# An mLSTM and mixture-of-experts kernel: its opening in a new order, with the scores of four tiles in paired row halves

## Chip, cores and metric

The kernel runs on one core of a Trainium2 chip, in one launch that computes the whole chain of three layers. The metric is the device time of one execution in microseconds (us); the median over several runs is given. The layout of the inputs (transposed copies, the gates repeated for each row group, the weights in blocks) is made on the host ahead of the launch and is not part of the time.

## The reference, cut to what is computed

Sizes: B=2 sequences of S=768 tokens, 8 heads of 40 columns, so 1536 tokens of 320 columns. First comes an mLSTM attention step by step over the tokens, then a mixture of 4 experts (320 to 1024 and back), then a gated feed-forward layer (320 to 1536 and back).

```python
def _attn_ref(q, k, v, i_gate, f_gate, o_gate):
    m = np.full((B, H), -1e+30)            # C, n start at zero
    for t in range(S):
        kt, vt, qt = k[:, :, t], v[:, :, t], q[:, :, t]
        m_new = np.maximum(f_gate[:, :, t] + m, i_gate[:, :, t])
        f_stab = np.exp(f_gate[:, :, t] + m - m_new)
        i_stab = np.exp(i_gate[:, :, t] - m_new)
        m = m_new
        C = f_stab * C + i_stab * np.einsum('bhd,bhe->bhde', vt, kt)
        n = f_stab * n + i_stab * kt
        h_tilde = np.einsum('bhde,bhe->bhd', C, qt)
        denom = np.maximum(np.abs(np.einsum('bhd,bhd->bh', n, qt)), 1.0)
        y[:, :, t] = sigmoid(o_gate[:, :, t]) * h_tilde / denom
    return y

def _moe_ref(x, domain_probs, w1, w2):
    p = domain_probs / (domain_probs.sum(-1, keepdims=True) + 1e-09)
    for e in range(E):
        out += p[:, e:e + 1] * (np.maximum(x @ w1[e], 0.0) @ w2[e])
    return out

def _moe2_ref(x, w_a, w_b, w_out):
    return ((x @ w_a) * (x @ w_b)) @ w_out
```

## The kernel before, in words

**Tiles.** The tokens are cut into 12 tiles of 128, numbered n = 2j+b: j (0 to 5) is the stretch of 128 tokens and b the sequence. Both tiles of one j go through the main products together, as 256 columns. The step-by-step attention is done in chunks: within a tile as a 128x128 matrix of scores times weights for each head, and from tile to tile through a state that is carried on.

**Attention of one tile.** The gates of a stretch j give running sums (gate0 and gate1 L379 to L389, gate_f L393 to L396, gate_i L400, gate2 L402 to L409, gate_c L415). Their result L is split into a rounded part (hi_L, hi_cm, L429) and a rest (low_L L442, low_cm L446). build_R (L475 to L482) spreads it over the heads in the tile's buffer Rr, four heads at a time ("half" hh = 0 or 1 of a tile); the lower rows of Rr are filled once (fill_R, L670). weights_of (L486 to L492) is one TensorE product of LT and Rr, w_exp (L497) its exponent on ScalarE, w_mask (L505) the causal mask on GpSimd. scores (L507 to L513) are four products of keys and queries in fp32, on 120 rows: for tiles 0 and 1 64 rows come from memory, and rows 64 to 120 are set to zero (zero_qk, L336); tiles 2 and 3 use the same buffers again and load 40 rows over them. s1b (L517, VectorE) multiplies scores and weights, s2a (L519 to L527) multiplies by the values, s2x (L550 to L562, VectorE) divides and applies the output gate og, whose sigmoid is o_gate (L362). s2c (L610, ScalarE) copies the last 64 columns of x once more, s3a (L145 to L147) transposes x on TensorE, and x_hi (L133, ScalarE) and x_lo (L136 and L138, VectorE) split it into a rounded and a rest part, xh and xl. Later tiles (from j=2 on) get their weights another way and are not touched by the change.

**Main products.** The 72 items k = 0 to 71 stand for the products of expert weights and both tiles of one j, twelve items for each j (blocks 0 to 2 of the weights, four items a block; the other blocks follow after them for all tokens). Item k multiplies into psa (L208, eight products of 256 columns), VectorE and ScalarE split the result (L275 and L276), and the second product goes into psy (L287 to L289). Two pieces of 352 columns of weights feed an item; block 0 thus has eight pieces, f = 0 to 7. A piece is a small generator (piece1): the first step is a load (L87, 176 KB, queue SP), the second ScalarE's rounded copy (L91), the third the subtraction that gives the rest (L93), on VectorE or on GpSimd after a table (block 0: p p v p v v p p, block 1: p p p v p p p v, p for GpSimd). A pass of `go` takes each named piece one step further.

**Order.** Everything beside the main products is a list `ev` of (key, function, arguments), L679 on. It is sorted by its keys and issued in that order: keys below zero ahead of item 0 (the opening), a key of 2.4 within item 2. Each engine takes its instructions strictly in the order of issue, and each DMA queue (SP's for most loads, ScalarE's for some, GpSimd's for one kind) its loads. So an instruction that waits holds all behind it on its engine. warm_up (L626) issues products of zeros on TensorE, ten at first and one to four at a time further on. table (L633) is a tiny activation that has ScalarE load the table of a function. weigh_k (L571, GpSimd), state and state_add carry the state on.

The lines that matter most ahead of item 0 are these; the opening of the list before is in the diff below.

## Time and profile before

| | |
|---|---|
| time, median of 3 runs | 612.29 us (611.9 to 612.41) |
| span of the profiled execution | 609.31 us |
| TensorE (PE) busy | 598.1 us, 98% |
| VectorE (DVE) busy | 406.5 us, 67% |
| ScalarE (ACT) busy | 277.9 us, 46% |
| GpSimd (POOL) busy | 193.3 us, 32% |
| granted TensorE clock, slices of the page | 9 tenths or more in all 40 |

The span is that of the profiled execution, from its first instruction to its last; the runs' times include a little more around it, 2.98 us against the median. The shares are means over the whole span. The opening (up to 20.9 us) and the first items are a small part of it, so what happens there is read from the timeline of these stretches, not from the shares. The page's chain of work that ended last is TensorE's for 92% of the span.

### The profile page before, as it was taken

How to read it: one execution, taken by the hardware profiler on the slowest of the kernel's cores; microseconds unless marked ns; L12 is line 12 of the kernel's file. 1: busy time of each engine (PE TensorE's matmuls, PEld its weight loads, DVE VectorE, ACT ScalarE, POOL GpSimd, SP SyncE). 2: the span in 40 equal slices, each digit the busy share in tenths (PEclk: the TensorE clock that was granted, in tenths of full speed). 3: DMA queues.
4: the chain of work that ended last, by engine and by line, in shares of the span. 5: the costliest groups of instructions: out<-in, count | busy, mean ns of one | idle time of the engine just before them, and what ended most of it. 6: DMA issues, size and time to landing. Idle time of an engine off the chain costs nothing.

```text
span 609.3 us, 14397 instructions
## 1 busy us (share of the span) xinstructions
PE 598.1 (98%) x5815; PEld 564.5 (93%) x5815; DVE 406.5 (67%) x829; ACT 277.9 (46%) x643; POOL 193.3 (32%) x233
## 2 busy tenths in 40 slices
PE   8799999999999999999999999999999999999997
PEld 5699999999999899999999999988898988888886
DVE  6898868676553333333789899898776787864344
ACT  7687476756533323333344344454553434331211
POOL 5486426363501011334233333333222222310000
PEclk9999999999999999999999999999999999999999
DMA  8877463737202122222222222222111120200002
GB/s 247 214 219 202 128 181 103 197 104 200 58 19 64 39 62 80 72 75 79 56 76 69 63 75 56 59 63 65 47 50 45 38 56 20 60 16 1 2 31 100
DMA packets 29351, 51.63 MB, mean 85 GB/s; under 512 B 3485, under 2 KB 18117, under 8 KB 29285
## 3 DMA queue, kind: packets, MB, share of 16 engines
q1 hardware_dynamic: 15925, 26.32, 15.9%
q10 hardware_dynamic: 12448, 22.03, 13.2%
q0 software_dynamic: 912, 2.36, 1.4%
q8 instruction: 45, 0.74, 0.5%
q14 instruction: 21, 0.17, 0.1%
HBM read 47.92 MB, written 2.00 MB: 82 GB/s over the span
## 4 chain that ended last, share of the span: by engine, by line
PE 92%; DVE 3%; POOL 1%; issue 1%; DMA 1%; ACT 1%; SPq 0%; DVEq 0%; POOLq 0%
PE psy L253 27%; PE psa L228 27%; PE psb L228 11%; PE psa L208 10%; PE psy L287 3%; PE psy L289 3%; PE psy L288 3%; PE pt_y L527 3%; PE pt_c L513 1%; PE pt_i L533 1%; POOL wl L93 1%; PE pt_u L583 1%; DMA acc<-in_w1b 1%; PE pt_x L145 0%; DMA gt<-in_gates 0%
## 5 line engine op out<-in xcount | busy, mean ns | idle before, releaser
L228 PE MATMUL psa<-xh,wh 64*128 64x512 f32 x576 | 135.2, 390 | 0.0
L253 PE MATMUL psy<-wl,hh 64*128 64x320 f32 x752 | 131.3, 305 | 0.0
L253 PE MATMUL psy<-wh,hh 64*128 64x320 f32 x752 | 131.3, 305 | 0.0
L253 PE MATMUL psy<-wh,hl 64*128 64x320 f32 x752 | 131.2, 305 | 0.0
L228 PE MATMUL psa<-xh,wl 64*128 64x512 f32 x414 | 97.4, 389 | 0.0
L253 PEld LDWEIGHTS psy<-wh,hh 64*128 64x128 f32 x752 | 85.7, 184 | 0.8
L228 PEld LDWEIGHTS psa<-xh,wh 64*128 64x128 f32 x576 | 80.9, 184 | 5.9 <-issue 0.9
L253 PEld LDWEIGHTS psy<-wl,hh 64*128 64x128 f32 x752 | 85.5, 184 | 0.8
L253 PEld LDWEIGHTS psy<-wh,hl 64*128 64x128 f32 x752 | 85.7, 184 | 0.0
L228 PE MATMUL psa<-xl,wh 64*128 64x512 f32 x384 | 85.6, 389 | 0.0
L828 DVE SCALAR_TENSOR_TENSOR hl<-psa,hh 128x512 fp32r<-128x512 f32 x60 | 38.6, 685 | 55.2 <-ACT hh L827 54.9
L125 POOL TENSOR_TENSOR wl<-tp,lf 128x272 fp32r<-128x272 f32 x48 | 38.8, 809 | 113.1 <-DVE tp L124 111.4
L228 PE MATMUL psb<-xh,wh 64*128 64x512 f32 x216 | 69.8, 389 | 0.0
L228 PEld LDWEIGHTS psa<-xh,wl 64*128 64x128 f32 x414 | 60.7, 184 | 3.7
L228 PE MATMUL psb<-xh,wl 64*128 64x512 f32 x180 | 58.5, 389 | 0.0
L228 PEld LDWEIGHTS psa<-xl,wh 64*128 64x128 f32 x384 | 55.2, 184 | 3.6
L122 POOL TENSOR_TENSOR lf<-lf,sq 128x272 f32<-128x272 f32 x48 | 38.1, 794 | 62.9 <-ACT wh L121 48.9
L276 DVE SCALAR_TENSOR_TENSOR hl<-psa,hh 128x256 fp32r<-128x256 f32 x72 | 30.3, 421 | 40.4 <-ACT hh L275 40.0
L93 POOL TENSOR_TENSOR wl<-raw,wh 128x352 fp32r<-128x352 f32 x28 | 26.4, 947 | 95.1 <-ACT wh L91 68.6
L275 ACT ACTIVATE hh<-psa 128x256 fp32r<-128x256 f32 x72 | 27.6, 383 | 59.2 <-PE psa L208 58.5
L827 ACT ACTIVATE hh<-psa 128x512 fp32r<-128x512 f32 x60 | 32.6, 596 | 44.7 <-PE psy L253 26.6
L208 PE MATMUL psa<-xh,wh 128*128 128x256 f32 x216 | 51.5, 293 | 0.3 <-ACT xh L133 0.3
(146 smaller groups left out, 1435.1 us busy)
## 6 DMA issues: line engine op xcount, KB each, us to landing
raw<-in_w2b ACTq DMA_DIRECT2D x48, 272.0 KB, 2.8
...
```

The lines of the kernel that those rows point to most:

```text
L93: lo_eng.tensor_tensor(wl[:, cs], raw, wh[:, cs].bitcast(F32), op=ALU.subtract)
L122: nc.gpsimd.tensor_tensor(lf, lf, sq, op=ALU.mult)
L125: nc.gpsimd.tensor_tensor(wl[:, cs], tf, lf, op=ALU.add)
L208: nc.tensor.matmul(ps, l, r, start=(i == 0), stop=(i == len(prs) - 1))
L228: return nc.tensor.matmul(ps[g], w[rows, o:o + P], x, start=start, stop=stop)
L253: ms = [nc.tensor.matmul(ps[t], l[rows, t * P:(t + 1) * P], w[rows, off:off + DM], start=start, stop=stop) for t, rows in zip(two, (UP, DN))]
L275: nc.scalar.activation(self.hh, ps, AF.Relu)
L276: nc.vector.scalar_tensor_tensor(self.hl, ps, 0.0, self.hh.bitcast(F32), op0=ALU.max, op1=ALU.subtract)
L287: nc.tensor.matmul(ps, lh, wh[:, off:off + DM], start=(fi == 0), stop=False)
L288: nc.tensor.matmul(ps, lh, wl[:, off:off + DM], start=False, stop=False)
L827: nc.scalar.activation(hh, ps[f], AF.Relu)
L828: nc.vector.scalar_tensor_tensor(hl, ps[f], 0.0, hh.bitcast(F32), op0=ALU.max, op1=ALU.subtract)
```

## The change

The list's opening is written anew, and some of the functions it calls are changed:

- **Loads.** The keys and queries of tiles 0 to 3 are loaded as 48 rows a half (RQ), both halves of a tile in one buffer, one from partition 0 and one from partition 64; there is no zero_qk any more. The loads for the second halves of tiles 0 and 1 go on ScalarE's queue. og of j=0 is the third load on SP's queue, ahead of tile 1's first half.
- **Scores.** scores2(n) issues the eight products of a tile's two halves in turns, the one from rows 0 to 39, the other from rows 64 to 103, each into a bank of its own. It serves tiles 0 to 3. Tile 2's stand ahead of item 0, tile 3's at 5.343.
- **ScalarE.** Sigmoid's table is loaded first, then both fills of Rr, then the sigmoid of og 0, then hi_L, then Exp's table. The exponents of tiles 0 and 1 stand in a row of four. Exp's table is not asked for between a sigmoid and the exponents of the next gates in the opening; the entry at 0.678 stays.
- **Gates to GpSimd.** hi_cm of j=0 goes from ScalarE to GpSimd, and so does the first half of tile 1's Rr; the four slices of Rr that ScalarE made go to VectorE as one build of four heads.
- **x of tiles 0 and 1.** The quotient goes into a buffer of its own (xu), and GpSimd multiplies its last 64 columns by og a second time into x; ScalarE's copy of these columns (s2c) is not called for j=0.
- **Moves.** gate0, gate1 and gate_f of j=1 stand in the opening. The first ten warm_up products stay, the later ones go. All pieces of block 0 are done ahead of item 0, w1's first two pieces get both further steps at 1.21 to 1.24. gate_tail 1 goes from 2.939 to 3.8, gate_out 1 from 3.684 to 3.85.

The functions:

```diff
@@ load_qk @@
-            if 2 <= n < NP:
-                t["qk", hh] = td[n - 2]["qk", hh]
+            if n < NP:
+                if "two" not in t:
+                    tag, bufs = ("qs", 2) if n == NP - 1 else ("qk", QB)
+                    t["two"] = qp.tile([KS, 2, 512], F32, tag=tag, name="qk_t", bufs=bufs)
+                at, r, to = 64 * hh, RQ, t["two"]
             else:
-                tag, bufs = ("qs", 2) if (n, hh) == (1, 1) else ("qk", QB)
-                t["qk", hh] = qp.tile([KS, 2, 512], F32, tag=tag, name="qk_t", bufs=bufs)
-            v = t["qk", hh].rearrange("p a b -> p (a b)")
-            r = 64 if n < 2 else D if n < NP else KS
-            (eng or nc.sync).dma_start(v[0:r], qk[n, hh, 0:r])
+                to = t["qk", hh] = qp.tile([KS, 2, 512], F32, tag="qk", name="qk_t", bufs=QB)
+                at, r = 0, KS
+            v = to.rearrange("p a b -> p (a b)")
+            (eng or nc.sync).dma_start(v[at:at + r], qk[n, hh, 0:r])
@@ scores2, new @@
+        def scores2(n):
+            t = td[n]
+            for hh in range(2):
+                t["pc", hh] = ps_t.tile([P, 512], F32, tag="t", name="pt_c")
+            for h in range(4):
+                hs = slice(h * P, (h + 1) * P)
+                for hh in range(2):
+                    v = t["two"][64 * hh:64 * hh + D]
+                    nc.tensor.matmul(t["pc", hh][:, hs], v[:, 1, hs], v[:, 0, hs], start=True, stop=True, skip_group_check=True)
@@ s2x @@
-            nc.vector.tensor_tensor(xv, y[:, :, 0:D], dn.to_broadcast([P, H, D]), op=ALU.mult)
-            t["last"] = nc.vector.tensor_tensor(xv, xv, r, op=ALU.mult).ins
+            if j == 0:
+                xu = a2.tile([P, H, D], F32, tag="y", name="xu_t", bufs=1)
+                nc.vector.tensor_tensor(xu, y[:, :, 0:D], dn.to_broadcast([P, H, D]), op=ALU.mult)
+                nc.vector.tensor_tensor(xv, xu, r, op=ALU.mult)
+                nc.gpsimd.tensor_tensor(x[:, DM:], xu.rearrange("p h d -> p (h d)")[:, 256:DM], og[j][:, b, 256:DM], op=ALU.mult)
+            else:
...
```

The opening of the list (loads of constants and most pieces of weights left out):

```diff
-            (-110, load_gates, 0, nc.sync), (-109, load_rsel, nc.scalar), (-108, load_qk, 0, 0, nc.sync), (-107, load_qk, 0, 1, nc.scalar),
-            (-106, load_qk, 1, 0, nc.sync), (-105, load_qk, 1, 1, nc.sync), (-102.626, zero_qk, 0, 0, V), (-100.942, table, AF.Exp),
...
-            (-68, scores, 0, 0), (-66.868, go, w0[5:6]), (-65.844, scores, 0, 1), (-65.387, gate1, 0),
...
-            (-62.277, hi_cm, 0, nc.scalar), (-62.241, low_L, 0), (-61.301, load_gates, 1), (-60.985, build_R, 0, V, 0, 4), (-60.522, low_cm, 0),
-            (-59.112, build_R, 1, V, 4, 8), (-57.494, build_R, 1, V, 0, 4), (-57.303, fill_R, 1), (-56.721, load_qk, 2, 1),
-            (-56.674, build_R, 0, nc.scalar, 4, 8), (-55, weights_of, 0, 0, ps_b, "b"), (-55, w_exp, 0, 0), (-55, w_mask, 0, 0),
...
+            (-40, load_gates, 0, nc.sync), (-39.9, load_rsel, nc.scalar), (-39.8, load_qk, 0, 0, nc.sync), (-39.7, load_qk, 0, 1, nc.scalar),
+            (-39.6, load_o, 0, nc.sync), (-39.5, load_qk, 1, 0, nc.sync), (-39.4, load_qk, 1, 1, nc.scalar), (-39.3, load_kvo, 1), (-39.2, load_kvo, 0),
+            (-39.1, load_v, 0), (-39, table, AF.Sigmoid), (-38.9, ones), (-38.8, fill_R, 0), (-38.7, fill_R, 1), (-38.6, gate0, 0), (-38.5, warm_up, WARM),
...
+            (-35, scores2, 0), (-34.9, o_gate, 0), (-34.8, gate1, 0), (-34.7, gate_f, 0, V), (-34.6, gate_i, 0, nc.gpsimd), (-34.5, gate2, 0),
+            (-34.4, gate_c, 0, V), (-34.3, hi_L, 0, nc.scalar), (-34.2, hi_cm, 0, nc.gpsimd), (-34.1, low_L, 0), (-34, table, AF.Exp),
+            (-33.9, low_cm, 0), (-33.8, build_R, 0, V, 0, 4), (-33.7, build_R, 1, nc.gpsimd, 0, 4), (-33.6, build_R, 0, V, 4, 8), (-33.5, build_R, 1, V, 4, 8),
+            (-33.4, scores2, 1), (-33, weights_of, 0, 0, ps_b, "b"), (-32.9, w_exp, 0, 0), (-32.8, w_mask, 0, 0), (-32.7, weights_of, 0, 1, ps_b, "b"),
+            (-32.6, w_exp, 0, 1), (-32.5, w_mask, 0, 1), (-32.4, weights_of, 1, 0, ps_a, "a"), (-32.3, w_exp, 1, 0), (-32.2, w_mask, 1, 0),
+            (-32.1, weights_of, 1, 1, ps_b, "b"), (-32, w_exp, 1, 1), (-31.9, w_mask, 1, 1),
+            (-31.8, s1b, 0, 0), (-31.7, s1b, 0, 1), (-31.6, s2a, 0, 0), (-31.5, s2a, 0, 1), (-31.4, s1b, 1, 0), (-31.3, s1b, 1, 1),
+            (-31.25, gate0, 1), (-31.24, gate1, 1), (-31.2, s2a, 1, 0), (-31.1, s2a, 1, 1), (-31, go, w0[0:1]), (-30.9, go, w0[1:2]), (-30.8, gate4, 0), (-30.7, gate5, 0),
...
+            (-30.4, go, w0[0:1]), (-30.3, go, w0[1:2]), (-30.2, s2b, 0), (-30.1, s2x, 0), (-30, s3a, 0), (-29.9, x_hi, 0), (-29.85, go, w0[3:4]), (-29.8, s2b, 1), (-29.7, s2x, 1),
+            (-29.6, go, w0[2:3]), (-29.5, go, w0[4:5]), (-29.4, go, w0[5:6]), (-29.3, x_lo, 0), (-29.2, s3a, 1), (-29.1, x_hi, 1), (-29.05, gate_f, 1, V), (-29, x_lo, 1),
+            (-28.8, go, w0[6:7]), (-28.7, go, w0[7:8]), (-28.6, go, w0[4:5]), (-28.5, go, w0[5:6]), (-28.48, go, w0[6:7]), (-28.47, go, w0[7:8]), (-28.45, scores2, 2),
+            (-28.4, load_qk, 3, 0), (-28.3, load_qk, 3, 1), (-28.2, load_kvo, 2), (-28.1, load_o, 1, nc.sync),
+            (-28, go, w1[0:1]), (-27.9, go, w1[1:2]), (-27.8, go, w1[2:3]), (-27.7, go, w1[4:5]), (-27.6, go, w1[3:4]), (-27.5, load_gates, 2), (-27.4, go, w1[5:6]),
```

Behind item 0's key the list keeps its order but for the moves named above: scores of tile 2 at 2.182 and 2.31 and of tile 3 at 5.343 and 5.623 become scores2 2 in the opening and scores2 3 at 5.343, and the passes of w0[6], w0[7], gate0 1, gate1 1 and gate_f 1 from -1.439 to 0.618 stand in the opening.

## Rows read from the trace of the kernel before

**Rows 1.** The page's busy line: engine, busy us, share of the span, instructions.

```profile
PE 598.1 (98%) x5815; PEld 564.5 (93%) x5815; DVE 406.5 (67%) x829; ACT 277.9 (46%) x643; POOL 193.3 (32%) x233
```

**Rows 2.** Timeline of TensorE (start, us, engine, line, operation); one piece of the chain.

```profile
6.49 2.02 PE L513 MATMUL pt_c<-qk_t 120*128 120x128 f32 x16 [0.73 <-DVE cm L415]
...
8.27 0.48 PE L492 MATMUL pt_a<-Rr,LT 112*128 112x512 f32 x1
...
20.93 0.39 PE L208 MATMUL psa<-xh,wh 128*128 128x256 f32 x1 [0.27 <-ACT xh L133]
...
218.56 7.04 PE psy L253 x96
```

**Rows 3.** Table of stretches: us from the start, length, busy us by engine.

```profile
20.90:46.70 25.80, 24.63 (x192) 23.58 (x192) 24.29 (x52) 20.67 (x50) 19.24 (x19) 1.00 0.71 203
...
51.00:61.00 10.00, 10.00 (x81) 9.99 (x81) 7.52 (x17) 8.56 (x25) 4.98 (x7) 1.00 0.76 205
```

**Rows 4.** Waits to 60 us (TensorE) and from 20.9 to 47 us (VectorE).

```profile
DVE w_t L517 <- POOL w_t L505: 0.6, 1, 0.6
...
PE pt_y L527 <- DVE w_t L517: 0.4, 1, 0.4
```

**Rows 5.** Timeline of VectorE (DVE) and GpSimd (POOL) where they meet and where not.

```profile
6.82 0.68 DVE L482 TENSOR_TENSOR Rr<-zx,rsel 64x512 fp32r<-64x512 f32 x1
...
28.54 1.10 DVE L482 TENSOR_TENSOR Rr<-zx,rsel 64x512 fp32r<-64x512 f32 x1
...
27.78 2.67 POOL L93 TENSOR_TENSOR wl<-acc,wh 128x352 fp32r<-128x352 f32 x2 [2.63 <-ACT wh L91]
...
55.03 1.29 POOL L353 TENSOR_TENSOR qs_t<-qk_t,qs_t 40x512 fp32r<-40x512 f32 x1
```

**Rows 6.** Timeline of ScalarE (ACT) in the opening.

```profile
1.24 0.54 ACTq L334 DMA_DIRECT2D qk_t<-in_qk  x1
...
1.81 1.28 ACT L633 ACT_TABLE_LOAD   x1 [1.81 <-issue]
...
3.33 1.04 ACT L670 CAST Rr<-rsel 48x1024 fp32r<-48x1024 f32 x1
...
6.05 0.30 ACT L429 CAST zh<-L 64x128 fp32r<-64x128 f32 x1 [1.68 <-DVE L L409]
...
8.88 1.28 ACT L497 ACTIVATE w_t<-pt_a 128x512 f32<-128x512 f32 x2
...
14.81 0.74 ACT L363 ACTIVATE og_t<-og_t 128x640 f32<-128x640 f32 x1
```

**Rows 7.** Table of stretches (its last column GB/s moved) and landing of qk_t's loads.

```profile
3.60:7.60 4.00, 3.27 (x16) 1.64 (x15) 3.25 (x10) 2.22 (x4) 0.71 (x2) 1.00 1.05 215
...
8.60:12.60 4.00, 3.72 (x30) 3.44 (x29) 1.93 (x4) 3.12 (x9) 1.79 (x3) 1.00 1.08 369
...
DMA to landing us min/median/max: 6.1/6.1/6.1
```

**Rows 8.** Timeline of VectorE and GpSimd up to the first main product.

```profile
3.94 0.49 DVE L389 TENSOR_TENSOR_SCAN mr<-gt,mr 112x128 f32<-112x128 f32 x1 [0.48 <-DMA gt<-in_gates]
...
4.79 0.38 DVE L396 TENSOR_TENSOR lf<-lf,mr 112x128 f32<-112x128 f32 x1
...
7.54 0.35 DVE L446 SCALAR_TENSOR_TENSOR LT<-zh,rsel,cm 48x128 fp32r<-48x128 f32 x1
...
9.60 1.26 POOL L505 TENSOR_SCALAR_AFFINE_SELECT w_t<-w_t 128x512 f32<-128x512 f32 x2 [4.58 <-ACT w_t L497]
...
12.75 1.29 DVE L517 TENSOR_TENSOR w_t<-pt_c,w_t 128x512 f32<-128x512 f32 x2 [1.16 <-POOL w_t L505]
...
18.05 0.17 DVE L556 TENSOR_SCALAR dn_t<-pt_y 128x8 f32<-128x8 f32 x1
...
19.21 0.49 DVE L562 TENSOR_TENSOR x_t<-x_t,og_t 128x320 f32<-128x320 f32 x1
...
19.62 0.95 DVE L93 TENSOR_TENSOR wl<-acc,wh 128x352 fp32r<-128x352 f32 x2
```

More of the change, by code (lines that the diff above doesn't have):

```diff
@@ L37 @@
 QB = 3
+RQ = 48
 WARM = 10
@@ L684, in mlstm_moe_kernel @@
-            (-79.066, gate0, 0), (-76.45, load_v, 1), (-75.79, load_o, 0, nc.sync), (-75.176, go, w0[4:5]), (-74.955, zero_qk, 1, 1, nc.gpsimd),
-            (-74.482, load_mask), (-74.114, load_k, 0), (-73.514, go, w0[6:7]), (-73.345, go, w0[7:8]), (-70.77, fill_R, 0), (-70.643, warm_up, WARM),
-            (-70.226, load_k, 1), (-69.676, load_dp), (-68, scores, 0, 0), (-66.868, go, w0[5:6]), (-65.844, scores, 0, 1), (-65.387, gate1, 0),
-            (-64.959, gate_f, 0, V), (-64.541, gate_i, 0, nc.gpsimd), (-63, gate2, 0), (-63, gate_c, 0, V), (-62.343, hi_L, 0, nc.scalar),
@@ L700, in mlstm_moe_kernel @@
-            (-11.457, go, w1[2:3]), (-11.296, x_hi, 1), (-8.738, x_lo, 1), (-8.052, go, w0[6:7]), (-6.827, warm_up, 1), (-5.408, go, w1[4:5]),
-            (-4.663, go, w0[5:6]), (-3.504, go, w0[7:8]), (-3, go, w1[3:4]), (-1.824, load_gates, 2), (-1.494, go, w1[5:6]), (-1.439, gate0, 1),
-            (-1.41, gate_tail, 0), (0.4, gate1, 1), (0.4, gate_i, 1, V), (0.5, go, w0[6:7]), (0.511, gate_f, 1, V), (0.618, go, w0[7:8]), (0.678, table, AF.Exp),
-            (0.985, gate_out, 0), (1.209, go, w1[6:7]), (1.45, gate2, 1), (1.45, gate_c, 1, V), (1.45, hi_L, 1, nc.scalar), (1.45, hi_cm, 1, V),
@@ L704, in mlstm_moe_kernel @@
-            (1.512, low_L, 1), (1.512, low_cm, 1), (1.517, build_R, 2, V, 0, 4), (1.581, weigh_k, 0), (1.6, gate4, 1), (1.6, gate5, 1), (1.685, go, w1[1:2]),
-            (1.735, go, w1[1:2]), (2.013, go, w1[0:1]), (2.182, scores, 2, 1), (2.31, scores, 2, 0), (2.439, build_R, 2, V, 4, 8), (2.518, go, w1[0:1]),
-            (2.699, weigh_k, 1), (2.829, weights), (2.835, go, w1[2:3]), (2.89, go, w1[2:3]), (2.939, gate_tail, 1), (3.11, go, w1[3:4]), (3.419, go, w1[3:4]),
-            (3.497, go, w2[0:1]), (3.684, gate_out, 1), (3.814, go, w1[4:5]), (3.871, weights_of, 2, 0), (3.9, w_exp, 2, 0), (3.9, w_mask, 2, 0),
+            (-40, load_gates, 0, nc.sync), (-39.9, load_rsel, nc.scalar), (-39.8, load_qk, 0, 0, nc.sync), (-39.7, load_qk, 0, 1, nc.scalar),
@@ new lines, in mlstm_moe_kernel @@
+            (-28.8, go, w0[6:7]), (-28.7, go, w0[7:8]), (-28.6, go, w0[4:5]), (-28.5, go, w0[5:6]), (-28.48, go, w0[6:7]), (-28.47, go, w0[7:8]), (-28.45, scores2, 2),
+            (-28.4, load_qk, 3, 0), (-28.3, load_qk, 3, 1), (-28.2, load_kvo, 2), (-28.1, load_o, 1, nc.sync),
+            (-28, go, w1[0:1]), (-27.9, go, w1[1:2]), (-27.8, go, w1[2:3]), (-27.7, go, w1[4:5]), (-27.6, go, w1[3:4]), (-27.5, load_gates, 2), (-27.4, go, w1[5:6]),
+            (-1.41, gate_tail, 0), (0.4, gate_i, 1, V), (0.678, table, AF.Exp),
@@ new lines, in mlstm_moe_kernel @@
+            (0.985, gate_out, 0), (1.209, go, w1[6:7]), (1.21, go, w1[0:1]), (1.22, go, w1[1:2]), (1.23, go, w1[0:1]), (1.24, go, w1[1:2]), (1.45, gate2, 1), (1.45, gate_c, 1, V), (1.45, hi_L, 1, nc.scalar), (1.45, hi_cm, 1, V),
+            (1.512, low_L, 1), (1.512, low_cm, 1), (1.517, build_R, 2, V, 0, 4), (1.581, weigh_k, 0), (1.6, gate4, 1), (1.6, gate5, 1), (2.439, build_R, 2, V, 4, 8),
+            (2.699, weigh_k, 1), (2.829, weights), (2.835, go, w1[2:3]), (2.89, go, w1[2:3]), (3.11, go, w1[3:4]), (3.419, go, w1[3:4]),
@@ L711, in mlstm_moe_kernel @@
             (4.718, go, w1[6:7]), (4.995, state, 0), (5, state_in, 0), (5, state_add, 0), (5.122, go, w2[3:4]), (5.123, o_gate, 1), (5.153, go, w2[1:2]),
-            (5.236, go, w2[5:6]), (5.255, go, w2[0:1]), (5.26, s1b, 2, 1), (5.343, scores, 3, 1), (5.35, state_old, 1), (5.411, go, w1[7:8]),
+            (5.236, go, w2[5:6]), (5.255, go, w2[0:1]), (5.26, s1b, 2, 1), (5.343, scores2, 3), (5.35, state_old, 1), (5.411, go, w1[7:8]),
             (5.445, go, w2[7:8]), (5.45, state, 1), (5.45, state_in, 1), (5.5, s2a, 2, 0), (5.523, load_kvo, 3), (5.55, gate1, 2), (5.55, gate_f, 2, V),
-            (5.6, s2a, 2, 1), (5.623, scores, 3, 0), (5.655, go, w2[0:1]), (5.716, table, AF.Exp), (5.78, s2b, 2), (5.78, load_o, 2, nc.sync),
+            (5.6, s2a, 2, 1), (5.655, go, w2[0:1]), (5.716, table, AF.Exp), (5.78, s2b, 2), (5.78, load_o, 2, nc.sync),
             (5.879, go, w2[3:4]), (5.891, go, w2[5:6]), (5.9, s2x, 2), (5.9, weights_of, 3, 0), (5.9, w_exp, 3, 0), (5.9, w_mask, 3, 0), (5.932, go, w2[4:5]),
```

26 lines of the change are left out of this document (10 added, 16 removed).

## The prediction

> **What bounds the kernel now.** I began with the page's busy shares [rows 1]: TensorE works 98% of a span of 609.3 us. Such a kernel gains only where TensorE waits, or when it is given less to do, and then only if nothing else ends last. On TensorE's own timeline [rows 2] the first main product starts at 20.93 us; what stands before it is the opening that the change rewrites.
>
> The second question is whether an earlier first product reaches the end. The table of stretches [rows 3] answers it. From 20.9 to 46.7 us VectorE is busy about 24.5 of 25.8 us, as full as TensorE; from 51 to 61 us it is busy 75% and TensorE all the time. The waits [rows 4] confirm it: in the first stretch VectorE stands still 0.6 us for anything longer than a cast, while TensorE's last stop there, 0.4 us, is for VectorE's product of weights and scores (tile 3). So from 20.9 to 46.7 us VectorE sets the pace, and after it TensorE. TensorE work saved before 46.7 us is worth no more than its waits there; what counts is when VectorE finishes its list.
>
> Third, why VectorE is so full: it takes turns with GpSimd. The build of Rr (L482) takes 0.68 us at 6.82, with GpSimd idle, and 1.10 us at 28.54, where GpSimd works on the pair of L93 that began at 27.78 [rows 5]. The Trainium skill, "SBUF — State Buffer", section "SBUF: two separate sides", calls this an exclusive lock on a shared port pair, held for the whole instruction. The trace agrees in kind (1.10 against 0.68 us); by the rule alone every meeting costs the rest of GpSimd's operation, and the change, which sets more GpSimd work beside VectorE's early chain, would pay for it.
>
> **The change, part by part.** I follow the chain to the first main product and write each term as after minus before.
>
> *Sigmoid first.* Before, ScalarE loads Exp's table at 1.81 us, fills Rr once (1.04) and is free when L is ready: hi_L starts at 6.05 [rows 6]. After, it first issues one more load (0.54, as at 1.24), then come table and dummy (1.81 to 3.33, so 1.52), two fills (2.08) and the sigmoid (0.74) ahead of hi_L: 1.81+0.54+1.52+2.08+0.74=6.7 if no data is late. The sigmoid needs og, now third on SyncE's queue. By about 3.6 gates are through (VectorE has them at 3.94, rows 8); of what comes ahead of og, or beside it from ScalarE's queue, two score loads of 192 KB are then left, and og's 320 KB. The trace has two rates: 215 GB/s in the stretch of score loads, 369 GB/s later [rows 7]. 704 KB take 1.9 or 3.3 us, to 5.5 or 6.9. From the last bytes to the semaphore I estimate 0.4 to 1.1 us, since a score load takes 6.1 us to land there [rows 7]. So og lands between 5.9 and 8.0; I take 6.6, nearer the early end as og itself is of the later, faster kind. hi_L then starts at 6.6+0.74+0.05=7.4: **+1.35** (bounds +0.65 and +2.7). The Trainium skill ("SBUF — State Buffer", section "Can I just issue two DMAs to hit both halves?") says that two loads at a time, one at partition 0 and one at 64, gain 6% over one. By it the slow rate holds and og lands near 7.7, hi_L starts at 8.5; no stretch here has such a pair.
>
> *Half of tile 1's Rr on GpSimd.* No row before has it. The nearest is 40x512 on GpSimd, 1.29 us at 55.03 [rows 5]. It becomes ready with zx, just as VectorE is to build tile 0's first half, for which the first exponent waits. Taking turns, VectorE waits: **+1.0** (bounds 0 and +1.3; I go by the long end, since the 28.54 row waited although most of GpSimd's operation had passed). In exchange ScalarE's four slices go, and the scores are done earlier: before, the first weight product starts at 8.27, behind 16 score instructions, with its operand ready at 7.54+0.35=7.89 [rows 2, 8]: **-0.35** (bounds 0 and -0.4).
>
> *Exponents in a row.* Before, from the first exponent at 8.88 to the end of the last of four products with scores, 12.75+1.29=14.04, are 5.16 us [rows 6, 8]. After, four exponents at 0.64 (1.28 for two) start 0, 0.64, 1.28 and 1.92 after the first; the last one ends 0.6 later, then come its mask (0.63, 1.26 for two), its product (0.65) and 0.3 of hops: 4.1 us, **-1.05** (bounds -0.6 and -1.3).
>
> *Both tiles' x.* Before, from 14.04 to the end of tile 1's x (19.21+0.49=19.70) are 5.66 us [rows 8]; tile 0's sigmoid and casts stand between. After, VectorE does the next gates' scan (0.49) and twice the five steps of a tile (18.05 to 19.70, so 1.65): 3.8, and 0.3 for turns with GpSimd: **-1.55** (bounds -1.9 and -0.8).
>
> *From x to the first product.* 1.23 us before (19.70 to 20.93). ScalarE's copy of 64 columns goes; a GpSimd product takes its place, beside VectorE's. Tile 2's scores now stand on TensorE ahead of the first main product: 16 instructions at 0.11 (2.02 us for 16, with a tail), 0.9 us when they run in pairs, against some 0.55 until the casts are done: **+0.35** (bounds 0 and +1.25).
>
> The sum: 1.35+1.0-0.35-1.05-1.55+0.35=-0.25, so the first main product starts at about 20.7.
>
> *VectorE from there to 46.7 us.* It starts 0.25 earlier. The second gates' scan (0.49) and two sums (up to 0.38 each) are already done, 1.2 us; one more subtraction of block 0 falls behind the first product, 0.5 (0.95 for two) [rows 8]: net **-0.7**. Up to 27.78 GpSimd had been idle 2.63 us [rows 5], which left VectorE's chain of seven small operations alone. Now block 0's last pieces, block 1's first two and both weigh_k meet that chain. Four meetings at some 0.35 (the row's 0.42 and less for smaller ones) are +1.4; GpSimd is then ahead by as many pieces and meets VectorE less in the next 5 us, -0.8: net **+0.6** (bounds -0.4 and +1.6). The end of the stage: -0.25-0.7+0.6=**-0.35**.
>
> *What counts nothing.* Paired scores: half-row products run at 7.04/96=0.073 us [rows 2], where a full-row score instruction takes 0.11, so pairs in fp32 may save up to 0.9 us a tile (0 if they don't overlap). Tile 2's and tile 3's lie where VectorE ends last; with that cover gone they would be worth up to 1.8 us. The four zero fills go, but their engines wait for gates until 3.94 anyway. The single warm-ups lie in TensorE's idle time. ScalarE no longer reloads Exp's table in the main loop; its time is not what VectorE waits for [rows 4]. On SyncE block 1's first loads now stand behind tile 3's scores, tile 2's values and og 1; if they come late TensorE waits for their subtraction, 0 to +0.5.
>
> The profiled execution's span is 609.31 us, 2.98 below the median of 612.29; -0.35 on either gives **611.9 us**.
>
> **Rivals.** (A) GpSimd's turns cost little: VectorE's build of Rr starts first, and the later meetings balance. Then 1.0 and 0.6 go from the sum, and with og at 6.2 another 0.4: -2.35, **609.9**. For it: at 4.79 in the opening L396 took only 0.38 us beside a GpSimd operation [rows 8]. Against: rows 5, and VectorE's full stage [rows 3]. (B) The sigmoid's input is late. It is one load in front of ScalarE's order, and each microsecond delays hi_L and all behind it. At a landing of 8.6 the sum is -0.35+2.0: **613.9**. It decides from a landing at about 8.2 on (6.6+0.35+1.2). For it: 215 GB/s and 6.1 us to land in just this stretch [rows 7]. Against: fewer score bytes stand ahead of og than stood ahead of that load. (C) The pairs don't run side by side, so that part of the change does nothing. Then tile 2's scores hold the first product 0.9 us longer, of which VectorE's chain sees about half: **612.3**.
>
> **How the numbers follow.** 0.2%, or 1.2 us, is about what a measurement of this kernel can tell from no change. Chances: forecast 0.38 and C 0.05 (both within 0.2%), A 0.35 (faster), B 0.22 (slower). So faster 0.35, same 0.43, slower 0.22. The forecast alone runs from 611.1 to 613.3. For 8 in 10 the range goes into A as far as -2.9, with the x term near its low bound too, and into B as far as a landing at 8.7: 609.4 to 614.0.
>
> **What would show it.** hi_L at 7.4 with ScalarE waiting for og before it; the first build of Rr near 1.5 us beside a GpSimd build of about 1.3; the last product with scores 4.1 us after the first exponent, tile 1's x 4.1 us after that; the first main product near 20.7. Then the step on which all hangs: TensorE's stop of 0.4 us ahead of tile 3's second half grows to 2 us or so, because TensorE has less to do and VectorE arrives there hardly earlier. If that stop stays small and the stage ends 2 us earlier, VectorE did not bound it and the forecast is wrong on the fast side. If ScalarE waits for og past 8 us, it is wrong on the slow side; so it would be if the granted clock, 1.00 in each stretch of rows 3 (the 2.4 GHz level), fell below that now that the later warm-ups are gone.

## The result, and the profile after

The changed kernel takes **619.16 us** (median of four runs, 618.72 to 619.47) where the kernel before, measured beside it, takes 612.10 us: a ratio of 1.0122 (95% interval 1.0104 to 1.0141). The span of its profiled execution is 616.8 us, 7.5 more than before. The forecast was 611.9 with a range up to 614.0, so it was wrong: slower, as its rival B would have it, but by more than any of its rivals allowed.

First TensorE's timeline in the opening (columns as in [rows 2]): the answers to the scores, the first weight product and the first main product. The value products of tiles 0 and 1 (32 instructions) and tile 2's scores are added.

```profile
6.05 1.16 PE L515 MATMUL pt_c<-qk_t 40*128 40x128 f32 x16 [0.98 <-DMA qk_t<-in_qk]
...
11.17 2.25 PE L492 MATMUL pt_a<-Rr,LT 112*128 112x512 f32 x4 [1.06 <-DVE Rr L482]
...
14.13 7.12 PE L537 MATMUL pt_y<-kvo_t,w_t 128*128 128x82 f32 x32 [0.71 <-DVE w_t L527]
...
23.96 2.08 PE L515 MATMUL pt_c<-qk_t 40*128 40x128 f32 x16
...
26.10 0.78 PE L209 MATMUL psa<-xh,wh 128*128 128x256 f32 x2
```

The first main product starts at 26.10 us, 5.2 later than in [rows 2] and 5.4 later than forecast. The rows show why: 16 paired score instructions take 1.16 us at 6.05, and 2.08 at 23.96. The same work takes nearly twice as long. The table of stretches (columns as in [rows 3]; the third from last is the granted clock) says when:

```profile
4.00:8.00 4.00, 2.23 (x21) 1.24 (x19) 2.16 (x7) 1.88 (x3) 0.80 (x2) 1.00 1.06 264
...
8.00:12.00 4.00, 1.99 (x18) 1.58 (x19) 3.08 (x5) 2.33 (x5) 1.20 (x1) 0.87 1.09 318
...
11.00:28.00 17.00, 14.85 (x68) 12.75 (x69) 11.49 (x27) 6.92 (x17) 8.55 (x11) 0.50 0.83 226
...
28.00:47.00 19.00, 15.53 (x119) 14.07 (x118) 16.02 (x31) 12.86 (x33) 10.20 (x11) 1.00 0.47 140
```

The same first two stretches of before:

```profile
4.00:8.00 4.00, 3.27 (x18) 1.92 (x17) 3.56 (x11) 2.21 (x5) 0.51 (x1) 1.00 1.05 205
...
8.00:12.00 4.00, 3.72 (x29) 3.27 (x28) 2.52 (x4) 3.13 (x9) 1.26 (x2) 1.00 1.07 338
```

The granted clock is 0.50, the 1.2 GHz level, from about 11 to 28 us, where before the column reads 1.00 all the time. In the two stretches from 4 to 12 us, in the second of which it falls, TensorE was busy 2.23 and 1.99 of 4 us; before it was 3.27 and 3.72.

The second half of the loss is in VectorE's stage. Three views show it: TensorE's waits from 20 to 80 us (answering [rows 4]), the timeline of VectorE's chain ahead of tile 2's Rr (answering [rows 5]; before had 0.42, 0.29, 0.23, 0.34 and 0.35 for the five), and GpSimd's beside it:

```profile
PE pt_a L492 <- DVE Rr L482: 2.2, 1, 2.2
...
PE pt_y L537 <- DVE w_t L527: 0.4, 1, 0.4
```

```profile
30.16 1.06 DVE L409 TENSOR_TENSOR_SCAN L<-rmask,lf 112x128 f32<-112x128 f32 x1
31.25 0.86 DVE L415 TENSOR_TENSOR cm<-cm,L 48x128 f32<-48x128 f32 x1
32.15 0.70 DVE L429 CAST zh<-cm 48x128 fp32r<-48x128 f32 x1
32.88 0.78 DVE L442 SCALAR_TENSOR_TENSOR zx<-zh,rsel,L 64x128 fp32r<-64x128 f32 x1
33.69 0.93 DVE L446 SCALAR_TENSOR_TENSOR LT<-zh,rsel,cm 48x128 fp32r<-48x128 f32 x1
...
46.89 0.50 DVE L553 TENSOR_TENSOR y_t<-pt_i,ET 128x328 f32<-128x328 f32 x1 [1.75 <-PE pt_i L543]
```

```profile
29.99 1.97 POOL L94 TENSOR_TENSOR wl<-acc,wh 128x352 fp32r<-128x352 f32 x2 [2.87 <-ACT wh L92]
31.92 1.59 POOL L587 TENSOR_TENSOR kw_t<-kvo_t,ET 128x360 f32<-128x360 f32 x2
33.54 0.93 POOL L94 TENSOR_TENSOR wl<-acc,wh 128x352 fp32r<-128x352 f32 x1
```

Five small operations take 4.33 us instead of 1.63; beside them GpSimd works without a pause from 29.99 to 34.5, and with its pieces moved away they are short again (e5 below). TensorE stops 2.2 us for what comes behind them. VectorE's last row is a third thing: it stands 1.75 us for pt_i, the product of tile 2's query with the state, which it never did before at this place.

ScalarE (answering [rows 6]) shows the order of the opening: the sigmoid waits 2.12 us for og, which landed at 7.9.

```profile
7.90 0.74 ACT L363 ACTIVATE og_t<-og_t 128x640 f32<-128x640 f32 x1 [2.12 <-DMA og_t<-in_kvo]
...
8.54 0.28 ACT L429 CAST zh<-L 64x128 fp32r<-64x128 f32 x1
...
11.97 2.11 ACT L497 ACTIVATE w_t<-pt_a 128x512 f32<-128x512 f32 x4 [1.64 <-PE pt_a L492]
```

### The profile page after: what moved, and what is told of

Same layout as the page of the kernel before. It is cut to its first block, busy times and chain, and to the rows that moved or that the text cites. A ratio compares the mean times of both kernels' runs of the same rounds, so it can differ in the third digit from the quotient of the medians.

```text
span 616.8 us, 14371 instructions
## 1 busy us (share of the span) xinstructions
PE 600.9 (97%) x5808; PEld 566.6 (92%) x5808; DVE 406.6 (66%) x827; ACT 274.3 (44%) x636; POOL 192.2 (31%) x235
## 4 chain that ended last, share of the span: by engine, by line
PE 93%; DVE 4%; DMA 1%; ACT 0%; issue 0%; SPq 0%; POOL 0%; DVEq 0%; POOLq 0%
PE psy L254 27%; PE psa L229 26%; PE psb L229 11%; PE psa L209 10%; PE pt_y L537 4%; PE psy L288 3%; PE psy L290 3%; PE psy L289 3%; PE pt_i L543 1%; PE pt_c L523 1%; PE pt_u L599 1%; DMA og_t<-in_kvo 1%; DVE Rr L482 1%; PE pt_x L146 1%; DVE w_t L527 0%; PE pt_x L147 0%
## 5 line engine op out<-in xcount | busy, mean ns | idle before, releaser
L254 PE MATMUL psy<-wl,hh 64*128 64x320 f32 x752 | 128.6, 305 | 0.0
L254 PE MATMUL psy<-wh,hh 64*128 64x320 f32 x752 | 128.4, 305 | 0.0
L254 PE MATMUL psy<-wh,hl 64*128 64x320 f32 x752 | 128.4, 305 | 0.0
L254 PEld LDWEIGHTS psy<-wh,hh 64*128 64x128 f32 x752 | 83.0, 184 | 0.8
L254 PEld LDWEIGHTS psy<-wl,hh 64*128 64x128 f32 x752 | 82.8, 184 | 0.8
L254 PEld LDWEIGHTS psy<-wh,hl 64*128 64x128 f32 x752 | 82.8, 184 | 0.0
```

Of the source, the lines that this page charges most:

```text
L254: ms = [nc.tensor.matmul(ps[t], l[rows, t * P:(t + 1) * P], w[rows, off:off + DM], start=start, stop=stop) for t, rows in zip(two, (UP, DN))]
```

## The experiments

Times are medians. The kernel before was 611.47, 611.61, 611.74 and 611.62 us beside the four groups of runs (e1 to e4; e5, e7 to e9; e6, e10 to e12; e13 and e14). A run that is "filled" has products of zeros where TensorE would stand. The diffs show the entries of the list that differ, cut out of their lines.

**e1_fill: the clock alone.**

```diff
-(-34.9, o_gate, 0),
+(-34.95, warm_up, 7), (-34.9, o_gate, 0),
-(-33, weights_of, 0, 0, ps_b, "b"),
+(-33.3, warm_up, 4), (-33, weights_of, 0, 0, ps_b, "b"),
-(-29.9, x_hi, 0),
+(-29.95, warm_up, 3), (-29.9, x_hi, 0),
```

> The changed kernel with warm-up products put where TensorE stood between its ten warm-ups and the values' products: 7 behind scores2 0, 4 behind scores2 1, 3 behind tile 0's transposes. Theory T (the granted clock, which fell from 1.00 to 0.50 at 11 us and came back at 28 us, is the loss; it fell after a stretch from 5 to 11 us in which TensorE was busy 2.4 of 6 us): clock 1.00 throughout, the 32 values' products of tiles 0 and 1 near 3.7 us instead of 7.12, the first main product near 21.5 (forecast 20.7, and hi_L came 1.1 later than forecast), time 611.5 to 613.5. Rival R (late og and turns of VectorE and GpSimd are the loss, the clock only fills their waits): the clock holds and the time stays at 616 or more.

618.05 us (615.08 to 619.71): by time this is rival R, and 1.1 us below the changed kernel lies within the spread. In the profiled execution, the fastest of the four (615.1 us), theory T's rows are there: the value products take 3.80 us and the first main product starts at 21.35. But 3.6 us of the loss stay even there, and the clock falls once more, behind a stop for Rr (timeline, then a stretch with the clock third from last):

```profile
7.47 1.68 PE L642 MATMUL pt_w<-acc 128*128 128x512 bf16 x7
...
14.02 3.80 PE L537 MATMUL pt_y<-kvo_t,w_t 128*128 128x82 f32 x32 [0.98 <-DVE w_t L527]
...
30.43 0.67 PE L492 MATMUL pt_a<-Rr,LT 112*128 112x512 f32 x1 [1.86 <-DVE Rr L482]
...
25.66 1.07 DVE L409 TENSOR_TENSOR_SCAN L<-rmask,lf 112x128 f32<-112x128 f32 x1
26.77 0.70 DVE L415 TENSOR_TENSOR cm<-cm,L 48x128 f32<-48x128 f32 x1
```

```profile
32.00:36.00 4.00, 4.00 (x25) 3.83 (x24) 4.00 (x7) 3.14 (x8) 4.00 (x5) 0.75 0.37 100
```

So both theories are right in part: the clock is one loss, GpSimd's turns another, and the second brings the first back. The mean clock of the four executions was 0.995 (615.1 us), 0.994 (616.9), 0.984 (619.2) and 0.984 (619.7).

**e2_before_bare: the kernel before without its later warm-ups.**

```diff
-(-30.053, warm_up, 1), (-17.366, warm_up, 4), (-12.403, warm_up, 1), (-6.827, warm_up, 1),
```

> The kernel before without its later warm-up products (seven, at 13.4, 17.4 to 18.7 and 20.2 us and one beside), the first ten stay. Theory T: the fall in the changed kernel at 11 us lies ahead of the places of these products, so they were not what held it; here the clock stays 1.00 up to 13 us at least and the time is within 1 us of before if it stays so to 21 us. Rival W (the later warm-ups held the clock): it falls to 0.50 between 15 and 25 us, the first items run at half clock, +3 to +7 us.

611.52 us, ratio 0.9997 (0.9982 to 1.0011), with the clock at half from about 16.4 to 26.6 us (stretches, then the first main product on the timeline):

```profile
14.00:17.00 3.00, 1.44 (x10) 1.32 (x11) 1.92 (x6) 2.61 (x4) 2.36 (x3) 0.90 1.09 331
17.00:20.00 3.00, 2.13 (x11) 1.91 (x9) 1.45 (x6) 1.63 (x4) 0.38 (x1) 0.50 0.92 234
```

```profile
22.41 0.79 PE L208 MATMUL psa<-xh,wh 128*128 128x256 f32 x2 [0.41 <-ACT xh L133]
```

Rival W is right about the clock and wrong about the time. The removed warm-ups did hold the clock (a mean of 0.991 to 0.994 in e2's ten executions, 0.998 or more in the thirteen of before beside them); the first main product came 1.5 us later without them, and yet the time is the same. Most of that is found at 66 us, where TensorE in the kernel before stops for VectorE's split of tile 4's queries (waits):

```profile
PE pt_c L513 <- DVE qs_t L353: 1.2, 1, 1.2
```

This row isn't in e2's list. A delay of the opening up to about this size can be given back there; the 5 us of the changed kernel are too much for it.

**e3_old_warm: the old warm-ups back.**

```diff
+(-31.45, warm_up, 1), (-31.4, s1b, 1, 0),
+(-31.05, warm_up, 5), (-31, go, w0[0:1]),
+(-29.15, warm_up, 1), (-29.1, x_hi, 1),
```

> The changed kernel with the later warm-up products back where the kernel before had them (one within the values' products, five behind them, one behind tile 1's transposes). Theory T: the fall comes at 11 us all the same, ahead of them; half clock as long as in the changed kernel, give or take 2 us, time 617.5 to 619.5. Rival W: the clock stays or comes back before 20 us, time 612 to 614.

620.01 us, 0.5 above theory T's range and far from rival W's. Theory T holds in what it says of the old warm-ups: ahead of their places the value products run at the half rate again (16 in 3.71 us at 14.36, where e1 takes 3.80 for 32). But there is no fall at 11 us here. The ten warm-ups take 4.45 us, where e1's seven filled-in products of the same shape take 1.68, and the first 16 scores take 2.08: TensorE runs at the half rate from its first product on, to about 24 us. The clock column of this trace reads 1.00 throughout; the durations say otherwise, and they are what counts.

**e4_unpaired: the pairs.**

```diff
-            for h in range(4):
+            for hh in range(2):
-                for hh in range(2):
+                for h in range(4):
```

> The changed kernel with the eight products of each tile's scores half by half instead of in turns; same products, same banks. Theory P (pairs run side by side): 16 instructions take 1.8 to 2.0 us at full clock instead of 1.16, TensorE is busy some 1.5 us more between 5 and 11 us; the clock falls later or for less long, the time is 616 to 619.5. Rival C (pairs don't overlap, the 40 rows alone are what is quicker): again 1.16 us and 619 us.

621.05 us, slower than theory P's 616 to 619.5. At full clock 16 score instructions take 1.71 us unpaired and 1.16 paired, at half clock 3.09 and 2.08 (timeline). Pairs do run side by side, so rival C of the prediction is out. The clock fell in e4 too, and earlier: its column reads 0.51 from 8 to 12 us, after a stretch from 4 to 8 us in which TensorE was busy 3.04 of 4 us. So the pairing by itself isn't what lets it fall.

```profile
5.95 1.71 PE L515 MATMUL pt_c<-qk_t 40*128 40x128 f32 x16 [0.62 <-DMA qk_t<-in_qk]
...
24.75 3.09 PE L515 MATMUL pt_c<-qk_t 40*128 40x128 f32 x16
```

**e5_w1_late: GpSimd's pieces of block 1 back at their old keys** (on top of e1_fill).

```diff
-(1.21, go, w1[0:1]), (1.22, go, w1[1:2]), (1.23, go, w1[0:1]), (1.24, go, w1[1:2]),
+(1.685, go, w1[1:2]), (1.735, go, w1[1:2]), (2.013, go, w1[0:1]),
 (2.439, build_R, 2, V, 4, 8),
+(2.518, go, w1[0:1]),
```

> e1_fill with the casts and subtractions of block 1's first two pieces back at the keys they had before (1.685 to 2.518, behind the first build of Rr for tile 2, instead of 1.21 to 1.24). Theory G (what e1_fill still loses is GpSimd's work beside VectorE's chain of seven small operations ahead of tile 2's Rr: four of them took 0.53, 1.07, 0.70 and 0.70 us where before took 0.21, 0.42, 0.29 and 0.23): these four are short again, the first build of Rr for tile 2 begins some 1.9 earlier, TensorE's stop of 1.86 us for it all but goes, the clock does not fall there, time 611 to 613.5. Rival L (the meetings only move to the builds of Rr for tile 3 and the subtractions behind them): the time is 614.5 or more.

612.03 us, ratio to before 1.0012 (0.9997 to 1.0027): theory G. The operations are short again, and TensorE no longer stops for tile 2's Rr:

```profile
25.19 0.22 DVE L405 TENSOR_SCALAR lf<-lf 112x128 f32<-112x128 f32 x1
...
25.44 0.42 DVE L409 TENSOR_TENSOR_SCAN L<-rmask,lf 112x128 f32<-112x128 f32 x1
...
25.90 0.29 DVE L415 TENSOR_TENSOR cm<-cm,L 48x128 f32<-48x128 f32 x1
...
26.23 0.22 DVE L429 CAST zh<-cm 48x128 fp32r<-48x128 f32 x1
...
27.24 0.68 DVE L482 TENSOR_TENSOR Rr<-zx,rsel 64x512 fp32r<-64x512 f32 x1
...
40.28 0.50 DVE L553 TENSOR_TENSOR y_t<-pt_i,ET 128x328 f32<-128x328 f32 x1 [1.40 <-PE pt_i L543]
```

With these two edits the 7 us are gone, and VectorE still stands 1.40 us for pt_i.

**e6_w1_late_only: the same move with the clock left to fall** (the changed kernel with e5's edit and nothing filled in).

> The changed kernel with block 1's first two pieces at their old keys alone, no products filled in, so the clock falls at 11 us as in the changed kernel and the first main product is near 26. With e1_fill (618.05), e5_w1_late (612.03) and the changed kernel (619.16) it makes a square. If the two losses add, it lies 6 us below, which nothing in the traces bears out; theory: VectorE's chain of small operations is as long as before again (-1.9), but everything starts 4.7 late, of which the half clock gives nothing back: 615.5 to 617.5. Rival: with TensorE late, GpSimd's pieces fall elsewhere and nothing is won: 618.5 to 619.5.

617.33 us, within the theory's 615.5 to 617.5. The clock was low here from the first product on, as in e3, to about 31 us (the first 16 scores take 2.08 us, the 32 value products 7.12). The square is: changed 619.16; filled 618.05; moved 617.33; both 612.03. Alone the edits are worth 1.1 us, which isn't clear of the spread, and 1.8 us, together 7.1. The reason is in e1's rows: with GpSimd's pieces early, TensorE stops 1.86 us, and the clock falls there in place of the opening.

**e7_sig_late and e8_sig_late_R_vec: the sigmoid, and Rr on GpSimd** (on top of e5).

```diff
-(-39.6, load_o, 0, nc.sync),
-(-39, table, AF.Sigmoid),
-(-34.9, o_gate, 0),
-(-34, table, AF.Exp),
-(-30.8, gate4, 0), (-30.7, gate5, 0),
+(-39.05, load_o, 0, nc.sync), (-39, table, AF.Exp),
+(-31.97, gate4, 0), (-31.96, gate5, 0), (-31.95, o_gate, 0),
```

```diff
-(-33.7, build_R, 1, nc.gpsimd, 0, 4),
+(-33.55, build_R, 1, V, 0, 4),
```

> e5_w1_late with og 0 loaded behind the score loads and its sigmoid behind the four exponents (Exp's table first, as before). Theory S (og's landing at 7.9 us held ScalarE's rounded copy of L back by 2 us): the copy is at 6.6 instead of 8.54, the first main product at 19.6 to 20.2, time 1 to 2 us below e5_w1_late. Rival D (the opening then waits for something else, loads of values or of weights, or VectorE's stage takes no notice): within 0.6 us of e5_w1_late.

> e7_sig_late with the first half of tile 1's Rr on VectorE instead of GpSimd. In the changed kernel VectorE's three builds took 2.61 us with GpSimd's build of 1.20 beside the first, so about 0.6 over three times 0.68. If that is the price of taking turns, four builds alone take 2.72 and the first exponent comes 0.6 sooner, the fourth 0.1 later: time within 0.6 us of e7_sig_late either way. Rival: GpSimd's build costs VectorE nothing, then this is 0.5 to 0.8 slower.

614.45 and 614.39 us, 2.4 us slower than e5, so neither theory S nor rival D of e7 holds. The rounded copy did come at 6.28, 2.5 us sooner than in e5, but the first exponent only 0.5 (11.40 for 11.93): the weight products, whose operand is ready some 1.5 us after VectorE's first build begins (at 7.55 here, so about 9.1), stood on TensorE behind tile 1's scores and the filled-in products to 10.78. And that was lost again, since the multiplication by og took 1.09 us in place of 0.49, beside GpSimd's pieces; the first main product came at 22.00, where e5 has 21.42. A part of the 2.4 us is the clock: its mean is 0.994 or less in seven of e7's ten executions and in one of e5's; e7's two with 0.999 took 612.8 and 612.9 us.

```profile
6.28 0.30 ACT L429 CAST zh<-L 64x128 fp32r<-64x128 f32 x1 [0.50 <-DVE L L409]
...
8.99 1.16 PE L515 MATMUL pt_c<-qk_t 40*128 40x128 f32 x16
...
10.78 1.06 PE L492 MATMUL pt_a<-Rr,LT 112*128 112x512 f32 x3
...
16.84 1.09 DVE L574 TENSOR_TENSOR x_t<-xu_t,og_t 128x320 f32<-128x320 f32 x1
```

In e8's trace the clock is low at the first scores and comes up while the filled-in products run:

```profile
6.40 2.08 PE L515 MATMUL pt_c<-qk_t 40*128 40x128 f32 x16 [0.57 <-DMA qk_t<-in_qk]
...
8.41 2.78 PE L642 MATMUL pt_w<-acc 128*128 128x512 bf16 x7
...
11.11 1.16 PE L515 MATMUL pt_c<-qk_t 40*128 40x128 f32 x16
```

Who builds tile 1's first half makes no difference in time. VectorE's three builds take 2.62 us beside GpSimd's, four alone 2.49 in e8: GpSimd's half costs VectorE as much as it takes off it.

**e9_before_pairs and e11_before_pairs_late: the pairs alone, in the kernel before.** Tiles 2 and 3 load both halves into one buffer; scores2 2 stands at 2.182 and scores2 3 at 5.343 (e9) or 5.63 (e11).

> The kernel before with one part of the change alone: tiles 2 and 3 loaded as two row halves of one buffer and their scores in pairs, at the keys of their first scores. Forecast's theory (VectorE sets the pace from 20.9 to 46.7 us): TensorE's 16 instructions take 1.16 instead of 1.95 us for each tile, and the time is that of before within 0.7 us. Rival (TensorE sets it): 0.9 to 1.7 us faster.

> e9_before_pairs with the same move. e9 was 0.24% slower than before with TensorE's scores 0.8 us shorter for each tile, and its VectorE stood 1.40 us for pt_i at 39.2. Theory B: here it doesn't, and the time is that of before or up to 0.8 below it. Rival (the pair costs time elsewhere): again 0.2% slower.

e9: 612.93 us, ratio 1.0024 (1.0012 to 1.0037), slower although TensorE does less. e11: 611.32 us, 0.9994 (0.9979 to 1.0010). The difference is one key. In e9 the pair takes two of the pool's four banks at 5.343, so tile 2's product with values must wait for a bank that VectorE still reads, and VectorE then waits for TensorE (e9's rows, then e11's; that it is the bank is read from the order of the list, and the move of this one key takes the wait away):

```profile
36.97 1.12 PE L540 MATMUL pt_y<-kvo_t,w_t 128*128 128x82 f32 x8 [0.76 <-DVE w_t L530]
...
40.60 0.50 DVE L556 TENSOR_TENSOR y_t<-pt_i,ET 128x328 f32<-128x328 f32 x1 [1.40 <-PE pt_i L546]
```

```profile
39.46 0.49 DVE L556 TENSOR_TENSOR y_t<-pt_i,ET 128x328 f32<-128x328 f32 x1
```

Without the wait the pair is free, and worth nothing that can be measured, as the forecast said of a stage in which VectorE ends last.

**e10_banks: the same move on top of e5.**

> e5_w1_late with scores2 3 at 5.63 instead of 5.343, behind both of tile 2's products with values. Theory B: the pair takes two of the four banks of its pool at once, so the product with values of tile 2 (pt_y) gets the bank that s1b(2,1) has still to read; there it waits for VectorE's product to 36.6 us where before it began at 35.55, and VectorE then stands 1.40 us for pt_i at 38.9. With the pair behind it VectorE's wait is gone: 1.0 to 1.5 us faster than e5_w1_late, 610.5 to 611.2. Rival: the products of tile 3 then come late and VectorE waits for them instead: within 0.5 us of e5_w1_late.

612.47 us (609.89 to 613.65), against 612.03 for e5: by time alone inconclusive. The rows agree with the theory in part (VectorE's wait for pt_i at this place is gone; tile 2's xl starts at 46.23 instead of 47.62), and the four executions with a mean clock of 0.999 or more took 609.9 to 610.9 us, where e5's nine such took 611.7 to 614.2. So at equal clock the move gives about what the theory said, though four executions are few. In the other eight the clock was 0.991 to 0.996, and why it fell there more often than in e5 isn't known.

**e12_open, e13_open_bare, e14_w1_first: a better opening.** e12 is e10 with e7's edit and tile 1's scores behind the four weight products. e13 is e12 with nothing filled in. e14 is e12 with block 1's first two pieces loaded and subtracted ahead of VectorE's chain.

```diff
-(-33.4, scores2, 1), (-33.3, warm_up, 4), (-33, weights_of, 0, 0, ps_b, "b"),
+(-33, weights_of, 0, 0, ps_b, "b"),
-(-31.8, s1b, 0, 0),
+(-31.85, scores2, 1), (-31.84, warm_up, 4), (-31.8, s1b, 0, 0),
```

> e10_banks with og's load and sigmoid late (as e7_sig_late) and with the scores of tile 1 behind the four weight products instead of ahead of them. In e7 ScalarE's rounded copy came at 6.28 instead of 8.79, but the weight products, whose first operand was ready at 8.2, stood behind tile 1's scores (a load landing at 9.0) and four filled-in products to 10.78. Theory: without these ahead of them the exponents begin at 8.9 instead of 11.4, the first main product comes at 19.5 to 20.3 instead of 22.0, and the time is 0.5 to 1.5 us below e10_banks. Rival: block 1's weights, which land from 24.6 us on, hold VectorE's and TensorE's next step, and the time is that of e10_banks within 0.5 us.

> e12_open without its eleven filled-in products. Theory O (in the changed kernel the clock fell because TensorE stood for a late chain: og's landing, the sigmoid, and the fourth row's loads): with the chain 2 us earlier TensorE's own work from 6 to 16 us is denser and the clock holds or falls only after 15 us, time within 1.5 us of e12_open. Theory P (the paired scores alone leave TensorE too little to do): the clock falls near 11 us again, the first main product comes at 23 to 26 and the time is 2 to 5 us above e12_open.

> e12_open with block 1's first two pieces loaded ahead of tile 3's scores and cast and subtracted ahead of VectorE's chain of small operations, and the first weigh_k behind that chain. If the piece's subtraction, for which TensorE stops 1.2 us at item 4 in e12_open, is then through in time and no meeting comes in its place: 0.3 to 1 us faster than e12_open. Rival: GpSimd's two subtractions meet VectorE's first splits and sums instead, and VectorE bounds the stage anyway: within 0.4 us, or slower.

**e12 beats both kernels**: 610.81 us, ratio to before 0.9979 (0.9966 to 0.9992). The weight products start at 9.53, not at 8.2, since VectorE's first build lasts some 1.5 us beside GpSimd's, and the first main product at 20.93 instead of 19.5 to 20.3. Against e10 the gain is 1.7 us between the medians, and as far as the executions show it is the clock's: e12's nine executions with a mean clock of 0.999 or more have a median of 610.8 us, e10's four such 610.7. The chain came 0.55 us sooner than e10's 21.48, but TensorE stops 1.24 us at 65.7 for VectorE's split of tile 4's queries, as in e2's account, and e10's trace has no such stop.

```profile
9.53 1.68 PE L492 MATMUL pt_a<-Rr,LT 112*128 112x512 f32 x4 [1.01 <-DVE Rr L482]
...
13.10 3.70 PE L537 MATMUL pt_y<-kvo_t,w_t 128*128 128x82 f32 x32
```

e13 takes 615.80 us, by time theory P: though the chain is early, TensorE runs at half rate from its first warm-up on (ten in 4.45 us, the first 16 scores in 2.08) to 27 us, and the first main product comes at 25.23.

```profile
1.38 4.45 PE L642 MATMUL pt_w<-acc 128*128 128x512 bf16 x10 [1.38 <-POOL acc L637]
...
6.45 2.08 PE L515 MATMUL pt_c<-qk_t 40*128 40x128 f32 x16 [0.62 <-DMA qk_t<-in_qk]
...
13.26 7.12 PE L537 MATMUL pt_y<-kvo_t,w_t 128*128 128x82 f32 x32
...
25.23 0.78 PE L209 MATMUL psa<-xh,wh 128*128 128x256 f32 x2
```

So it isn't og's late landing alone that costs the clock; without the filled-in products the opening is slow with an early chain too. Up to its first scores e12 issues the same as e13 and has 10 warm-ups in 4.45 us as well, but its first 16 scores take 1.22 us: there the clock came up in time, here it didn't come up for another 20 us. Where it was late in a filled run, in e8, it came up during the filled-in products. Eleven products of zeros, which cost nothing themselves, are worth 5.0 us here. e14 takes 612.19 us: the stop of 1.2 us for block 1's first piece goes, and in its place TensorE stops 0.7 us for tile 2's Rr and 0.5 more for VectorE's products with scores. Its rival is right.

## Why the prediction was wrong, point by point

**The step that failed** is that the sum has no term for the clock. It prices every product of the opening at the full rate, and under "What counts nothing" it puts the removed warm-ups, and the work that shorter scores take from TensorE, at nothing or at a gain: "The single warm-ups lie in TensorE's idle time." A product of zeros costs nothing in idle time, but what it may hold is the clock, and I priced products by what they take, not by what they hold. I named the clock as something that would make the forecast wrong, and gave it neither a price nor a rival. Its price is 5.3 us (e6 to e5) or 5.0 (e13 to e12).

The reason that I gave there, "now that the later warm-ups are gone", isn't the right one either: in the kernel before their removal costs nothing (e2), and back in the changed kernel they don't help (e3). What of the change does cost the clock isn't isolated. It is not the pairing alone (e4) and not og's late landing alone (e13); the shorter scores (16 instructions in 1.16 us where the kernel before took 2.02), the waits for loads ahead of them and the new order are left, and no run has the changed order with scores of the old length. What is shown is the half rate itself, in the durations, and that products of zeros in the opening take it away.

**The chain to the first main product.** With the clock held (e5), the sum was 0.7 short, the first row 1.4 late and the next three each a little early, so that errors in part cancelled:

| step | forecast | changed kernel | e5 |
|---|---|---|---|
| rounded copy of L starts | 7.4 | 8.54 | 8.79 |
| from there to the first exponent | 3.5 | 3.43 | 3.14 |
| to the end of the last product with scores | 4.1 | 3.89 | 3.89 |
| to the end of tile 1's x | 4.1 | 7.15 | 3.83 |
| to the first main product | 1.6 | 3.09 | 1.77 |
| first main product | 20.7 | 26.10 | 21.42 |

The first row is 1.1 to 1.4 off: og landed at 7.9 to 8.1, at the late bound of my 5.9 to 8.0, not at 6.6. I took the fast end because og is of the later kind of load; it stands among score loads. Its rate was not the slow one all the same: the stretch from 3.60 to 7.60 moved 273 GB/s (239 in e5), against 215 before. At 273 the 704 KB take 2.6 us, to 6.2; the gates came 0.1 to 0.5 later than in [rows 8] (VectorE has them at 4.41, in e5 at 4.08), and the remaining 1.2 us are a little more than the longest way from the last bytes to the semaphore that the forecast allowed, 1.1. Whether other loads beside og have a part in them no run separates. The rule of the Trainium skill that stood there ("SBUF — State Buffer", section "Can I just issue two DMAs to hit both halves?") gave 7.7, near the landing. But that is no support for it: its gain is 6%, and the trace's stretch moved 27% more than before, e5's 11%, with other loads in the sum. Rival B, which begins at a landing of 8.2, was thus just missed. Its mechanism was tested by e7, and there a sigmoid out of the way brought the first exponent only 0.5 us forward; with tile 1's scores out of the way too (e12) the weight products started 1.9 us sooner than in e5. An order on TensorE that the forecast took as given was as much of a bound as ScalarE's.

**GpSimd's turns.** The term was "+0.6 (bounds -0.4 and +1.6)". In e1, where the clock is held in the opening, four operations of the chain take 3.00 us for 1.15, so +1.85, and the first build of Rr 1.38 for 0.68, +0.7; in the changed kernel five take 4.33 for 1.63. The mechanism was right and mis-sized: I counted four meetings at 0.35 and let GpSimd's lead give 0.8 back, but one operation after another met GpSimd, since its five went without a pause. By the rule of the Trainium skill, "SBUF — State Buffer", section "SBUF: two separate sides" (an exclusive lock, held for the whole instruction), each of the five would have waited for the rest of GpSimd's operation, an estimate of 0.6 to 0.8 us from where these start and end. The trace lies a little below it: 0.3 to 0.65 us for a meeting with operations of 0.8 to 1.0 us.

**The end of the stage.** "VectorE sets the pace" held where nothing new came: e11. The sign that the forecast hung on it didn't come all the same: TensorE's stop ahead of tile 3's second half stayed at 0.4 us. In the changed kernel TensorE came late to it; in e10, where it is 0.26, TensorE's slack went into earlier stops (0.74, 0.99 and 0.44 us). "VectorE sets the pace" failed where the new order turned the wait round. The pair of tile 3 holds two banks, TensorE's product with values waits for VectorE, and VectorE waits 1.40 us for TensorE: 1.6 us in time (e9 to e11). The forecast's list of what the pairing costs has no bank in it. The Trainium skill says it in "TensorEngine Tiling (Array Packing)", section "Gotcha 1: PSUM Pressure": row tiles write to different banks, so tiling needs more of them at once. The trace agrees, with these 1.40 us.

**What was right.** Pairs of fp32 products run side by side (1.16 for 1.71 us, e4), and are worth nothing in VectorE's stage. The forecast's 0.9 us a tile came out (2.02 to 1.16), but by luck in part: its 0.073 us was read off products of 320 columns, not 128, and of the 0.86 us pairs give 0.55; the other 0.31 is there with 40 rows unpaired (e4). The exponents in a row took 3.89 for the forecast 4.1, the two x 3.83 for 4.1. The first weight product came 1.55 us after VectorE's first build of Rr began, where the forecast had near 1.5 for that build. With the three losses repaired (e10), tile 2's xl starts at 46.23, 0.33 ahead of before's 46.56; the forecast had 0.35, from a first main product at 20.7 where e10 has it at 21.48, so the agreement is luck in part.

What stays open: what in the changed opening costs the clock, and why it falls more often in e10 than in e5.
